# A fused gated-linear-attention and MoE kernel: the first six blocks taken as pairs with 384-byte loads, and a program order written out as a list

## The chip, the cores and the metric

The kernel runs on one core of one Trainium2 chip, in one launch. The metric is the device time of that core in microseconds (us); lower is better. A core has five engines that run side by side, each with its own queue of instructions that it executes in order: TensorE (PE in the profile; its weight loads are PEld), VectorE (DVE), ScalarE (ACT), GpSimd (POOL) and SyncE (SP). In this kernel SP issues all the DMAs. An instruction that must wait for another engine, or for a DMA, holds up everything behind it in its own queue.

## What is computed

There are 4 sequences of 768 tokens with 8 heads of 48 channels. For each head a 48x48 state is decayed per channel and updated at every token, and the output is read from it with the query:

```python
for t in range(S):
    state = alpha[:, :, t, :, None] * state + np.einsum('bhd,bhe->bhde', k[:, :, t], v[:, :, t])
    y[:, :, t] = np.einsum('bhd,bhde->bhe', q[:, :, t], state)
...
x = y.transpose(0, 2, 1, 3).reshape(B * S, H * D)    # 3072 x 384
h = x @ w_in                                         # w_in 384 x 2048
g = s * np.maximum(h, 0.0) ** 2 + b
out = g @ w_out                                      # w_out 2048 x 384
```

All inputs and the output are float32. The four attention inputs are 4.7 MB each and lie in memory as (batch, head, token, channel), so that the 48 channels of one head and token are 192 contiguous bytes. The two weights are 3.1 MB each.

## The kernel before

**Blocks.** The work is cut into 24 blocks of 128 tokens, 6 for each sequence, with one token per partition. Block n goes through a chain of steps. `load` brings a, q, k and v of the block, each as one DMA with 1,024 pieces of 192 bytes. `st_ln` takes the logarithm of alpha; `st_cum` sums it over the tokens by a product with a triangular matrix, and also gives the block's whole decay; `st_exp_b` and `st_exp_i` make the decay factors and their inverses; `st_qb` and `st_kb` multiply them into q and k; `st_vcast` rounds v to bfloat16. Blocks 0 to 7 are transposed by TensorE (`st_T`) and copied back by DVE (`st_Tcopy`); later ones are transposed by a DMA (`st_Tdma`). `st_KV`, `st_t1` and `st_snew` carry the state from block to block. `st_A` makes the 128x128 scores of each head, `st_mask` cuts them to the causal half, `st_y` multiplies them with v and adds what the state gives, and `st_yevac` copies the result to `xd_sb` as the input of the dense layers.

**Dense layers.** Blocks are put together in groups of one or two (`GROUPS`). `mm1` computes one unit of the first dense layer: 512 columns of PSUM, which for a group of two is two of the 16 slices of 128 hidden channels. `relu` (ACT) and `square` (DVE) take it to `gt_sb`. `mm2` computes a quarter of the second layer for one block: four products of 384 columns. After four quarters `oevac` (DVE) scales and adds the bias, and `ostore` writes the block out. The bias is `b` times the column sums of `w_out`, made from `colsum_part`, `colsum_add`, `bias_mm` and `bias_copy`. The weights come in as eight DMAs of 768 KB (`load_w_in`, `load_w_out`) through four staging buffers, and ACT rounds them to bfloat16 (`cast_w_in`, `cast_w_out`).

**Order.** `Schedule` takes each step as an operation with an engine, an expected duration, a priority and the buffers that it reads and writes; it plays them through and then emits the instructions in the order found. The list `LOADS` gives the order of the first loads and of the weights. `fill` puts products with zeros into the gaps on TensorE before the first `mm2`. There are five input buffers for each of a, q, k and v (`NIN`).

Of the kernel before, what the change touches and what calls it, by code (L numbers as in the profile page):

```python
# [14 lines left out]

VW = 144

GROUPS = [2, 1, 1, 2, 2, 2, 2, 2, 2, 2, 2, 2, 2]
UNIT = 0.756
LEAD = {1: 98.3, 2: 224.9, 4: 115.8}  # L20

NPE = 8

NAY = 9

RING = 12

NST = 4

TB = 1.02  # L30
TW = 2.15
FILL_GAP = 0.45

P_BM, P_CS, P_BMM = -5, -380.7, 485.1
P = dict(
    ln=-4.98, cum=7.29, eb=-25.15, ei=-13.19, vc=29.56, qb=-11.01, kb=-39.87, T=15.87,
    Tc=-9.38, KV=-36.89, t1=-9.91, sn=53.95, Ay=-1.22, A=-16.47, mk=-35.05, y=52.89,
    ye=4.82, m1=-13.73, re=-0.8, sq=-9.48, m2=-14.41, oe=20.18,
)

LOADS = ["k1", "q1", "a1", "i0", "k2", "v1", "i1", "a2", "i2", "q2", "i3", "v2", "a3", "q3", "k3", "o0", "v3", "a4", "o1", "o2", "k4", "o3", "q4", "z0", "v4"]

class Schedule:
    HOP = 0.05

    def __init__(self):
        self.ops = []
        self.writer = {}
        self.readers = {}

    def op(self, eng, dur, prio, fn, *args, r=(), w=(), lat=0.08, lock=False):
        me = len(self.ops)
        deps = set()
        for x in r:
            if x in self.writer:
                deps.add(self.writer[x])
        for x in w:
            if x in self.writer:
                deps.add(self.writer[x])
            deps.update(self.readers.get(x, ()))  # L60
        for x in r:
            self.readers.setdefault(x, []).append(me)
        for x in w:
            self.writer[x] = me
            self.readers[x] = []
        self.ops.append((eng, dur, prio, fn, args, deps, lat, lock))

    def run(self):
        n = len(self.ops)
        end = [None] * n  # L70
        begin = [None] * n
        left = [len(o[5]) for o in self.ops]
        users = [[] for _ in range(n)]
        for i, o in enumerate(self.ops):
            for d in o[5]:
                users[d].append(i)
        free = {}
        ready = {}
        port = 0.0
        for i, o in enumerate(self.ops):  # L80
            free.setdefault(o[0], 0.0)
            ready.setdefault(o[0], [])
            if not left[i]:
                ready[o[0]].append((0.0, i))
        todo = n
        while todo:
            best = None
            for e, items in ready.items():
                if not items:
                    continue  # L90
                f = free[e]
                at = [(max(a, f, port if self.ops[i][7] else 0.0), self.ops[i][2], i) for a, i in items]
                t = min(at)[0]
                _, i = min((p, i) for a, p, i in at if a <= t + 1e-9)
                if best is None or t < best[0]:
                    best = (t, e, i)
            t, e, i = best
            ready[e] = [x for x in ready[e] if x[1] != i]
            eng, dur, _, _, _, _, lat, lock = self.ops[i]
            begin[i] = t  # L100
            free[e] = t + dur
            end[i] = t + dur
            if lock:
                port = t + dur
            todo -= 1
            for u in users[i]:
                left[u] -= 1
                if not left[u]:
                    a = 0.0
                    for d in self.ops[u][5]:  # L110
                        same = self.ops[d][0] == self.ops[u][0]
                        x = end[d] + (0.0 if same and eng == "PE" else self.ops[d][6])
                        a = max(a, x + (0.0 if same else self.HOP))
                    ready[self.ops[u][0]].append((a, u))
        self.begin, self.end = begin, end
        return begin

    def emit(self, fill, until):
        begin = self.run()
        free = 0.0  # L120
        for i in sorted(range(len(self.ops)), key=lambda i: (begin[i], i)):
            eng, _, _, fn, args = self.ops[i][:5]
            if eng == "PE":
                if fn is until:
                    free = None
                if free is not None:
                    if free > 0.0:
                        fill(begin[i] - free, free)
                    free = self.end[i]
            fn(*args)  # L130
# [3 lines left out]
def kernel(  # L134
# [13 lines left out]
    ctx.enter_context(tc.manual_schedule())  # L148

    B, H, S, D = q.shape  # L150
    C = 128
    NCH = S // C
    NP = H // 2
    NBLK = B * NCH
    d_model = moe_w_in.shape[0]
    d_ff = moe_w_in.shape[1]
    NJ = d_ff // 128
    NIN = 5

    sb = ctx.enter_context(tc.tile_pool(name="sb", bufs=1))  # L160
# [235 lines left out]
    def st_snew(n):  # L396
        if n % NCH in (0, NCH - 1):
            return
# [321 lines left out]
```

## Time and profile before

| | before |
|---|---|
| time, median of 3 runs | 194.94 us (193.78 to 196.74) |
| time of the profiled execution | 193.93 us |
| its span, first to last instruction | 192.0 us |
| granted TensorE clock, mean | 0.991 |
| PE busy | 175.3 us |
| PEld busy | 126.7 us |
| DVE busy | 135.9 us |
| ACT busy | 109.5 us |
| POOL busy | 33.3 us |
| DMA, all queues | 34.44 MB |

The time of an execution is 1.9 us longer than the span that the profile shows. Busy time counts an instruction from its start to its end, and instructions of PE and PEld are pipelined: they overlap one another, so a PE that is busy all the time need not be at its peak. In the page, strips of 40 digits show the busy share of an engine in 40 equal slices of the span, in tenths. "SPq" is SP's queue of DMA issues: a long time there is an issue that was held up. A group of instructions is named by its line in the kernel, its engine, and "output<-input" in the names of the tiles.

### The profile page before, as it was taken

The numbers are of one execution on the slowest core, as the hardware profiler recorded it, in microseconds if no ns is written. First come the engines' busy times: TensorE is split into PE (matmuls) and PEld (weight loads), VectorE is DVE, ScalarE is ACT, GpSimd is POOL, SyncE is SP. The second block draws the span as 40 slices with busy tenths as digits, with TensorE's granted clock in tenths as the row PEclk, the third lists the DMA queues.
The fourth block names the chain that finished last, engine by engine and source line by source line (L and its number), as shares of the span: only waits on it lengthen the run. The fifth ranks groups of instructions, "written<-read, shape, count | busy, mean of one in ns | idle before, by whom it ended". The sixth has DMA issues, their size and how long they took to land.

```text
span 192.0 us, 5369 instructions
## 1 busy us (share of the span) xinstructions
PE 175.3 (91%) x2153; PEld 126.7 (66%) x2153; DVE 135.9 (71%) x256; ACT 109.5 (57%) x225; POOL 33.3 (17%) x60
## 2 busy tenths in 40 slices
PE   1877688879999999999999999999999999999992
PEld 0555467657677767777777766776766876777761
DVE  4643299989799898877689868587777786554421
ACT  3254789984357847767475754763663763654300
POOL 8402022103120431201122313011131131000000
PEclk9996999999999999999999999999999999999999
DMA  6989979999999999999999998897998895011112
GB/s 122 203 219 317 312 161 245 353 223 205 196 232 193 219 140 213 197 214 188 196 160 209 145 236 188 171 207 169 208 197 195 164 180 144 3 43 41 40 45 82
DMA packets 124218, 34.44 MB, mean 179 GB/s; under 512 B 117536, under 2 KB 122656, under 8 KB 124192
## 3 DMA queue, kind: packets, MB, share of 16 engines
q1 hardware_dynamic: 124192, 34.09, 82.6%
q8 instruction: 17, 0.28, 0.6%
q14 instruction: 9, 0.07, 0.1%
HBM read 25.17 MB, written 4.72 MB: 156 GB/s over the span
## 4 chain that ended last, share of the span: by engine, by line
PE 66%; DMA 14%; DVE 8%; SPq 7%; ACT 2%; issue 1%
PE o_ps L515 29%; PE h_ps L490 25%; PE py_ps L444 5%; DMA wst<-in_moe_w_in_dram 4%; DMA q_in<-in_q_dram 4%; SPq L194 4%; DMA wst<-in_moe_w_out_dram 3%; PE a_ps L406 3%; SPq L240 3%; DMA qkT<-qk 3%; DVE am L415 2%; PE py_ps L364 2%; PE ct_ps L306 1%; DVE gt L506 1%; ACT r L499 1%
## 5 line engine op out<-in xcount | busy, mean ns | idle before, releaser
L490 PE MATMUL h_ps<-xd,w_in_bf 128*128 128x256 bf16 (+1 forms) x624 | 74.8, 264 | 0.8 <-ACT r L499 0.5
L499 ACT ACTIVATE r<-h_ps 128x512 bf16<-128x512 f32 x96 | 56.5, 601 | 32.3 <-PE h_ps L490 22.8
L515 PE MATMUL o_ps<-w_out_bf,gt 128*128 128x384 bf16 x384 | 72.8, 326 | 2.0 <-ACT w_out_bf L261 2.0
L490 PEld LDWEIGHTS <-w_in_bf 128*128 128x128 bf16 x624 | 54.7, 98 | 10.8 <-issue 1.2
L506 DVE TENSOR_TENSOR gt<-r 128x512 bf16<-128x512 bf16 x96 | 43.5, 465 | 21.7 <-ACT r L499 21.1
L515 PEld LDWEIGHTS <-gt 128*128 128x128 bf16 x384 | 36.0, 98 | 21.2 <-issue 2.3
L415 DVE TENSOR_TENSOR am<-a_ps,mask 128x1024 bf16<-128x1024 f32 x24 | 29.3, 1220 | 1.6 <-PE a_ps L406 1.4
L327 POOL CAST vp<-v_in 128x384 bf16<-128x384 f32 x24 | 13.3, 553 | 95.0 <-DMA v_in<-in_v_dram 84.7
L526 DVE SCALAR_TENSOR_TENSOR o_sb<-o_ps,s_col,bias_w 128x384 f32<-128x384 f32 x24 | 14.8, 616 | 10.0 <-PE o_ps L515 9.6
L300 ACT ACTIVATE la<-a_in 128x384 bf16<-128x384 f32 x24 | 12.5, 521 | 14.1 <-DMA a_in<-in_alpha_dram 13.9
L400 POOL TENSOR_TENSOR s_st<-t,blast 128x384 bf16<-128x384 bf16 x16 | 14.5, 909 | 30.8 <-DVE t L389 23.0
L468 ACT ACTIVATE xd<-py_ps 128x384 bf16<-128x384 f32 x24 | 11.8, 491 | 13.0 <-PE py_ps L444 12.8
L338 DVE TENSOR_TENSOR qk<-k_in,binv 128x384 bf16<-128x384 f32 x24 | 13.4, 558 | 6.7 <-ACT binv L323 5.5
L333 DVE TENSOR_TENSOR qk<-q_in,b_s 128x384 bf16<-128x384 f32 x24 | 13.5, 564 | 5.2 <-ACT b_s L320 4.1
L320 ACT ACTIVATE b_s<-ct_ps 128x384 f32<-128x384 f32 x24 | 11.7, 488 | 6.8 <-PE ct_ps L311 6.7
L389 DVE TENSOR_TENSOR t<-py_ps,s_st 64x192 bf16<-64x192 f32 x32 | 11.3, 353 | 3.9 <-PE py_ps L364 3.2
L306 PE MATMUL ct_ps<-la,U_bf 128*128 128x384 bf16 x24 | 8.0, 334 | 6.3 <-ACT la L300 6.3
L323 ACT ACTIVATE binv<-ct_ps 128x384 f32<-128x384 f32 x24 | 11.8, 490 | 0.0
L311 PEld LDWEIGHTS <-la 128*128 128x128 bf16 x96 | 6.0, 97 | 7.7 <-issue 5.6
L406 PE MATMUL a_ps<-qkT 64*128 64x128 bf16 x192 | 9.8, 222 | 1.0 <-DVE qkT L373 0.7
L406 PEld LDWEIGHTS <-qkT 64*128 64x128 bf16 x192 | 5.5, 96 | 7.3 <-issue 4.3
L444 PE MATMUL py_ps<-am,vp 128*32 128x128 bf16 x384 | 9.8, 224 | 0.5 <-DVE am L415 0.5
(42 smaller groups left out, 108.1 us busy)
## 6 DMA issues: line engine op xcount, KB each, us to landing
a_in<-in_alpha_dram SPq DMA_DIRECT2D x24, 192.0 KB, 3.9
q_in<-in_q_dram SPq DMA_DIRECT2D x24, 192.0 KB, 3.9
k_in<-in_k_dram SPq DMA_DIRECT2D x24, 192.0 KB, 3.9
v_in<-in_v_dram SPq DMA_DIRECT2D x24, 192.0 KB, 3.7
out_dram<-o_sb SPq DMA_DIRECT2D x24, 192.0 KB, 2.6
wst<-in_moe_w_in_dram SPq DMA_DIRECT2D x4, 768.0 KB, 8.4
wst<-in_moe_w_out_dram SPq DMA_DIRECT2D x4, 768.0 KB, 7.0
qkT<-qk SPq DMA_TRANSPOSE x16, 3.7
```

The source lines that it names most:

```text
L327: nc.gpsimd.tensor_copy(out=vp_sb[n % 4].rearrange("a p (x d) -> a p x d", d=D)[:, :, 0:3:2, :], in_=v_in[n % NIN].rearrange("a (p e) d -> ...
L333: nc.vector.tensor_tensor(out=qk_sb[n % 3][:, 0, :, 0:D], in0=q_in[n % NIN], in1=b_sb[n % 2], op=ALU.mult)
L338: nc.vector.tensor_tensor(out=qk_sb[n % 3][:, 1, :, 0:D], in0=k_in[n % NIN], in1=binv_sb[n % 2], op=ALU.mult,)
L400: nc.gpsimd.tensor_tensor(out=s_sb[n % 3], in0=t1_sb[n % 2], in1=bl, op=ALU.mult)
L406: nc.tensor.matmul(out=a_ps[:, e, p, :], lhsT=qkT[64 * e : 64 * e + 64, 1, p, :], rhs=qkT[64 * e : 64 * e + 64, 0, p, :], start=True, stop ...
L415: nc.vector.tensor_tensor(out=am_sb[n % 2].rearrange("a e p t -> a (e p) t"), in0=a_ps.rearrange("a e p t -> a (e p) t"), in1=mask.unsquee ...
L444: nc.tensor.matmul(out=y_ps[32 * (x % 4) : 32 * (x % 4) + 32, x // 4, :], lhsT=(st[:, p, c0 : c0 + 32] if e is None else vp[:, p, c0 + 48 ...
L490: nc.tensor.matmul(out=hp[:, i * n : (i + 1) * n], lhsT=w_in_bf[:, kk, 128 * j : 128 * (j + 1)], rhs=xd_sb[g % 3][:, kk, 0:n], start=(kk = ...
L499: nc.scalar.activation(out=r_sb[w % 2], in_=h_ps[w % 2], func=AF.Relu)
L506: nc.vector.tensor_tensor(out=gt_sb[:, js[0] : js[0] + len(js), c0 : c0 + n], in0=r, in1=r, op=ALU.mult)
L515: nc.tensor.matmul(out=op[:, 0:d_model], lhsT=gt_sb[:, j, c0 : c0 + C], rhs=w_out_bf[:, j, :], start=(j == 0), stop=(j == NJ - 1),)
L526: nc.vector.scalar_tensor_tensor(out=ots, in0=o_ps[(x // 4) % 2][:, 0:d_model], scalar=s_col, in1=bias_w, op0=ALU.mult, op1=ALU.add,)
```

## The change

The scheduler is gone. The order of all instructions is given by `PROGRAM`, a string of 897 items such as `mm1.0.6.0` (unit 6 of group 0 into PSUM bank 0) or `re.0.6.0.0.ACT`, which also name the engine for many steps. The other parts of the change are these:

- Blocks 0 to 5 are taken as three pairs of 256 tokens. Partition p holds the tokens 2p and 2p+1, so that a load (`ld2`) has pieces of 384 bytes; it brings two blocks with 1,024 pieces. The first half of the partitions is then the first block of the pair, the second half the second block. The steps ending in 2 handle such a pair: sums, scores and outputs are split by token parity `s` and by block `c`, and products that belong to one block use 64 rows of TensorE's array.
- From block 6 on, all transposes are DMAs (`T1`); blocks 6 and 7 were transposed by TensorE before. The three pairs are transposed by TensorE.
- All groups have two blocks; before there were two groups of one.
- Input buffers hold six blocks for each of a, q, k, v (before five); `gt` holds eight blocks (before twelve). Two weight loads are staged in `gt` buffers (`STAGE_GT`).
- The weights are rounded by ACT, DVE and POOL, and the column sums made by POOL and DVE. Some of the relu steps run on DVE, some of the squares on ACT or POOL, four of the first multiplications on POOL.
- Zero products to fill gaps stand at four places, as `F.26`, `F.33`, `F.19` and `F.16`, with 120 columns (before 45 products with 256 columns).
- A block of a pair is stored with two DMAs (`st`).

```diff
-GROUPS = [2, 1, 1, 2, 2, 2, 2, 2, 2, 2, 2, 2, 2]
-NPE = 8
-RING = 12
-LOADS = ["k1", "q1", "a1", "i0", "k2", "v1", "i1", "a2", "i2", "q2", "i3", "v2", "a3", "q3", "k3", "o0", "v3", "a4", "o1", "o2", "k4", "o3", "q4", "z0", "v4"]
-class Schedule:
...
+NPAIR = 3
+GROUPS = [2, 2, 2, 2, 2, 2, 2, 2, 2, 2, 2, 2]
+NIN = 6
+RING = 8
+STAGE = {0: 0, 1: 1, 2: 2, 3: 3, 6: 0, 7: 1}
+STAGE_GT = {4: 2, 5: 3}
+CUM_IN_H = [1]
+PROGRAM = """
+ld2.a.0 c_act c_U2 c_la.1 c_la.0 ld2.a.1 c_zeros ld2.v.0 c_half c_qk.0 ld2.q.0 c_t1.0 c_qk.1 c_mask2
+ld2.k.1 ld2.k.0 c_s.0 ld2.q.1 ln2.0 c_s.1 ld2.q.2 c_t1.1 ld_i.3 F.26 cum2.0.0 c_ident ld2.v.1 ln2.1
+cum2.0.1 c_U c_ones blk2.0 c_vp.1 eb2.0.1 cum2.1.0 c_s.2 ei2.0.0 cum2.1.1 c_vp.0 blk2.1 ei2.0.1
+vc2.0.1.POOL el2.0 vc2.0.0.DVE eb2.1.0 mul2.q.0.1.DVE ei2.1.0 eb2.1.1 el2.1 mul2.k.1.0.DVE ei2.1.1
+eb2.0.0 mul2.k.1.1.DVE mul2.q.0.0.DVE mul2.k.0.0.DVE F.33 T2.0.0 mul2.k.0.1.DVE mul2.q.1.1.POOL KV2.0
+ld1.k.7 Tc2.0.0.ACT ld_i.1 T2.0.1 t1.0 mul2.q.1.0.POOL ld_i.2 ld2.a.2 t1.1 ld1.k.6 Tc2.0.1.DVE ld_i.0
+ld2.k.2 sn.1.DVE F.19 A2.0.0 ld_o.0 A2.0.1 ci.3.POOL mk2.0.0 ld1.a.6 ld2.v.2 mk2.0.1 F.16 T2.1.0
+vc2.1.1.ACT vc2.1.0.POOL T2.1.1 Tc2.1.0.ACT Tc2.1.1.DVE y2.0 A2.1.0 ye.0.DVE ye.1.ACT A2.1.1 mk2.1.0
+KV2.1 ci.1.ACT mm1.0.6.0 t1.2 mm1.0.7.1 re.0.6.0.0.ACT ld_o.3 mk2.1.1 sn.2.POOL ld1.a.7 re.0.7.1.1.ACT
...
+sn.4.POOL ld1.q.6 sq.1.7.1.ACT mm1.1.6.1 mk2.2.1 ld1.q.8 cp.3.POOL re.0.1.0.1.ACT ld_bs co.1.DVE y2.2
+cp.1.POOL sq.0.1.1.DVE ye.5.ACT ye.4.DVE mm2.0.0 co.2.ACT ld1.v.8 re.1.6.1.1.DVE cum1.6 ld1.a.10
+mm1.2.5.0 sq.1.3.0.POOL cp.2.DVE ld1.q.7 mm1.2.0.1 ld1.a.8 ei1.6 ca.2.3.DVE ld1.v.6 ca.0.1.POOL mm2.0.1
...
+cum1.8 bc re.2.1.0.0.ACT mm1.2.7.1 vc1.6.POOL mul1.q.6.DVE eb1.8 mm1.2.4.0 oe.0 T1.6 sq.2.1.0.ACT KV1.6
...
+sn.7.POOL ld1.v.13 mk1.6 mm2.2.3 st.1 ei1.9 mm2.3.0 ld1.k.9 oe.2 ld1.q.9 cum1.10 Ay.7 ld1.k.11 eb1.10
...
+mm2.22.2 mm2.22.3 oe.22 st.22
+"""
...
+    def ld2(x, m):
+        b, c = 2 * m // NCH, 2 * m % NCH
+        nc.sync.dma_start(
+            out=whole(ins[x], m).rearrange("a s e -> a (s e)").rearrange("a (h f) -> a h f", h=H),
+            in_=src[x][b, :, c * C : (c + 2) * C, :].rearrange("h (p s) d -> p h (s d)", s=2),
+        )
...
+    def cum2(m, s):
+        l = whole(la, m)
+        for i in range(2):
+            nc.tensor.matmul(
+                out=b_ps(m, s)[:, 0 : H * D],
+                lhsT=U2x if i > s else U2,
+                rhs=l[:, i, :, 0:D],
+                start=(i == 0),
+                stop=(i == 1),
+            )
...
+        for p in range(NP):                                  # KV2
+            for s in range(2):
+                for c in cs:
+                    r = slice(64 * c, 64 * c + 64)
+                    nc.tensor.matmul(
+                        out=(py_ps, ct_ps)[c][:, 96 * p : 96 * p + 96],
+                        lhsT=kb[r, s, 128 * p : 128 * p + 128],
+                        rhs=v4[r, s, p, 0:3:2, :],
+                        start=(s == 0),
+                        stop=(s == 1),
+                    )
...
+        for p in range(NP):                                  # A2
+            for e in range(2):
+                r = slice(64 * e, 64 * e + 64)
+                for c in range(2):
+                    t = slice(64 * c, 64 * c + 64)
+                    nc.tensor.matmul(
+                        out=dst[t, e, 128 * p : 128 * p + 128],
+                        lhsT=T[r, s, 1, p, t],
+                        rhs=T[r, :, 0, p, t],
+                        start=True,
+                        stop=True,
+                    )
...
+        for i, (p, e, x) in enumerate(OWN):                  # y2
+            c0 = 32 * x - 96 * p + 48 * e
+            for s in range(2):
+                for c in range(2):
+                    r = slice(64 * c, 64 * c + 64)
+                    nc.tensor.matmul(
+                        out=y_out((py_ps, ct_ps)[c], x),
+                        lhsT=v2[r, s, p, c0 : c0 + 32],
+                        rhs=a2[r, s, e, p, :],
+                        start=(i < 4 and s == 0),
+                        stop=(i >= 12 and s == 1 and c not in states),
+                    )
...
+    def re(g, u, w, i, eng="ACT"):
+        if eng == "ACT":
+            nc.scalar.activation(out=r_sb[i], in_=h_ps[w], func=AF.Relu)
+        else:
+            nc.vector.tensor_scalar(
+                out=r_sb[i], in0=h_ps[w], scalar1=0.0, scalar2=None, op0=ALU.max
+            )
...
+    def sq(g, u, i, eng="DVE"):
+        r = r_sb[i].rearrange("a (j t) -> a j t", j=4 // GROUPS[g])
+        if eng == "ACT":
+            nc.scalar.activation(out=unit_out(g, u), in_=r, func=AF.Square)
+        else:
+            on(eng).tensor_tensor(out=unit_out(g, u), in0=r, in1=r, op=ALU.mult)
...
+    def F(n):
+        for _ in range(n):
+            nc.tensor.matmul(
+                out=h_ps[1][:, 392:512], lhsT=zeros[:, 0:128], rhs=zeros[:, 0:120], start=True, stop=True
+            )
+
+    ops = dict(locals())
+    for item in PROGRAM.split():
+        name, *args = item.split(".")
+        ops[name](*(int(x) if x.lstrip("-").isdigit() else x for x in args))
```

In the items of `PROGRAM`, `ld1`, `ld2`, `ld_i`, `ld_o` and `st` are loads and stores; `ci` and `co` round a quarter of `w_in` or `w_out`; `cp` and `ca` make the column sums; `bm`, `bmm` and `bc` the bias; `ln`, `cum`, `blk`, `eb`, `ei`, `el`, `vc`, `mul`, `KV`, `t1`, `sn`, `A`, `mk`, `y`, `ye` are the attention steps in the order told above, with 2 for a pair and 1 for a single block; `T2` and `Tc2` transpose a pair; `Ay.n` is the scores of block n followed by the output of block n-1; `re`, `sq`, `oe` are `relu`, `square` and `oevac`.

## The prediction

> **What bounds the kernel now.** I read the page first, for the busy shares over the span.
>
> ```profile
> span 192.0 us, 5369 instructions
> PE 175.3 (91%) x2153; PEld 126.7 (66%) x2153; DVE 135.9 (71%) x256; ACT 109.5 (57%) x225; POOL 33.3 (17%) x60
> ...
> PE   1877688879999999999999999999999999999992
> ...
> DMA  6989979999999999999999998897998895011112
> ...
> q1 hardware_dynamic: 124192, 34.09, 82.6%
> ```
>
> PE never pauses after the tenth slice (48 us); before, it is short of work while the DMA engines are already full. So the middle is bound by PE, the first quarter by loads. The chain of waits says which loads:
>
> ```profile
> 8.80 4.49 SPq L240
> 13.87 8.26 DMA wst<-in_moe_w_in_dram
> 22.15 1.49 ACT w_in_bf L248
> ...
> 25.47 6.15 DMA wst<-in_moe_w_out_dram
> ...
> 34.60 8.07 DMA q_in<-in_q_dram
> ...
> 47.73 2.11 PE o_ps L515 x12
> ...
> 55.64 1.31 PE h_ps L490 x12
> ...
> 180.67 7.81 PE o_ps L515 x48
> ```
>
> Until 47.7 us the path hangs on weights and inputs in turn; then products follow one another to the end. The last rows are prices: a unit of `mm1` is 0.655 us (1.31 for two), a quarter of `mm2` 0.65 (7.81 for twelve). The windows say how much PE lacks:
>
> ```profile
> 20.00:25.00 5.00, 3.85 (x38) 3.08 (x38) 1.94 (x4) 4.30 (x8) 0.00 (x0) 1.00 0.97 264
> 40.00:45.00 5.00, 4.17 (x63) 3.37 (x61) 4.56 (x9) 3.03 (x5) 0.95 (x1) 1.00 0.95 180
> 60.00:80.00 20.00, 20.00 (x275) 14.64 (x273) 18.32 (x36) 13.41 (x31) 6.00 (x8) 1.00 1.02 191
> ```
>
> The columns are length, busy time (count) of PE, PEld, DVE, ACT and POOL, clock, DMA share, GB/s. Around 20 us DVE is idle; by 40 us DVE and DMA are full and PE is not.
>
> **PE's sum before.** From the timeline, a block costs 0.35 us (`st_cum`), 0.17 (`st_KV`), 0.33 (`st_A`), 0.51 (`st_y`; 0.34 without a state), 0.45 more if PE transposes it. The first `mm1` starts at 21.0, after two blocks. From there: `mm1` 88 x 0.655 + 8 x 0.75 (groups of one) = 63.6; `mm2` 96 x 0.65 = 62.4; 22 blocks 29.1; six transposes 2.7; bias 1.4; together 159.2. PE ends at 188.5, so 8.3 us are waits and filling, nearly all before 50 us; 3.5 us of evacuation and store end the span.
>
> **DMA prices.** The packet records give means of 15.6 ns for 192 bytes, 27.4 for the 256 of a transpose, 73.5 for 1,536 and 97.5 for 2,048. Over 16 engines that is 1.00 us for a load of 1,024 packets, 1.75 for a transpose, 0.59 for a store, 2.35 for a weight. Packets overlap a little:
>
> ```profile
> 3.71 0.52 ACT L300 ACTIVATE la<-a_in 128x384 bf16<-128x384 f32 x1 [1.70 <-DMA a_in<-in_alpha_dram]
> 9.34 0.52 ACT L300 ACTIVATE la<-a_in 128x384 bf16<-128x384 f32 x1 [3.52 <-DMA a_in<-in_alpha_dram]
> ```
>
> Six loads land between these two logarithms, 0.94 us each, so I scale all by 0.95: load 0.95, transpose 1.67, store 0.56, weight 2.23. Data starts at 1.8 us, and a landing is seen 1.0 after its last byte.
>
> **Pair loads.** No packet of 384 bytes is in the trace. Below: the count of packets sets the price, 0.95 us a pair. Above: the bytes, two loads, 1.9. The straight line from 192 to 1,536 gives 23.9 ns, x 64 packets an engine x 0.95 = 1.45; I take this, being between two measured sizes. Twelve pair loads then save 12 x (1.90 - 1.45) = 5.4 us, in the stretch where the queue is the bound.
>
> The Trainium skill (DMA: Bandwidth & Descriptors, Specifications) asks for 512 bytes for line rate and has smaller transfers read, modified and written; 384 would stay on the bad side with 192. If that means the same price per byte, the pairs gain nothing, and the sum below is 5.4 us longer. The trace has no size between 256 and 1,536 that could show such a step.
>
> **When the dense layers start.** The sixth pair load (k of pair 0) lands at 1.8 + 6 x 1.45 + 1.0 = 11.5. The exponentials (eight of 0.39) are done by 10. Then one after another: two multiplications 1.0, `KV2` 0.5, `t1` twice 1.45, `Tc2` 0.6, `A2` 0.5, two masks 2.4, `y2` 1.6, `ye` 0.5, `KV2` 0.5 with handovers: 20.8. `ci.3` is on POOL from 16 to 18, covered by the masks. So the start is where it was, but four blocks are nearly through instead of two. At 0.95 a pair it would be 19.4 (the exponentials limit), at 1.9, 23.6.
>
> **What else moves.** Eighteen relus go to DVE: at least 0.42 us each (its square of the same tile), at most 0.83 (0.62 for 384 columns from PSUM, by size); I take 0.65, nearest the second: 12 us. Squares leave DVE: 15 to ACT (a relu's 0.60 at most), 8 to POOL (0.83 by size, 1.1): 23 x 0.46 = 11 off DVE. That is even, and hidden in the middle by what PE has queued, since DVE there keeps 8% free in the fullest window; in the ramp DVE's work is part of the walk below. Groups of one go: 8 x (0.75 - 0.655) = 0.8 off PE, in its sum. New waits stand on SP: `ld1.k.7` waits for the last multiplication of pair 0 (12.5 us), with all weights but one behind it, but at that time the queue still has three transfers (to 16 us); `ld_o.2` waits for `ci.0` on POOL (29), and SP comes to it at about 33; `ld_o.0` and `ld_o.1`, staged in `gt`, only hold up the squares of group 2, which come after 41. At nothing, all of them; without that cover, each us on SP is one of the queue. The sixth input buffer lets loads run further ahead, which only helps.
>
> **64-row products.** `y2` has 64 products of 64x32 and 24 for the states. Now 16 of 128x32 take 0.33 us, by overlapping. Below: the same 21 ns and less for the states, 1.5; above: nothing overlaps, 53 ns (128 columns at the rate of 0.65 us for 1,536), 88 x 53 = 4.7. I take 1.6, since the products stay in four column groups; a pair is then 0.64 (`cum2`) + 0.2 + 0.9 (`T2`) + 0.5 + 1.0 (`A2`) + 1.6 = 4.8 (upper end 8.7).
>
> **PE's sum after.** From the first `mm1`: 96 x 0.655 = 62.9; 62.4; 18 single blocks 23.5; bias 1.4; `y2` of pair 1, 1.6; pair 2, 4.6: 156.4. Walking the list to `y2.2` by hand, I find 3 us of waits: `re.0.3` on DVE behind `mk2.1.1`, `co.0` waiting for a weight, `cum2.2` behind `ye.3`. 20.8 + 156.4 + 3 + 3.5 = 183.7.
>
> **The queue's sum after.** `A1.6` needs `T1.6`, queued behind 12 pair loads (17.4), eight weights (17.8) and 17 loads (16.2), itself 1.67: 53.1 + 1.8 + 1.0 = 55.9. What PE has from there (72 `mm1`, 86 `mm2`, 18 blocks less their first sums) is 125.3: end 55.9 + 125.3 + 3.5 = 184.7. The same for `Ay.19`: 17.4 + 17.8 + 72 x 0.95 + 14 x 1.67 + 14 x 0.56 = 134.8, at 137.6; left are 24 `mm1`, 33 `mm2` and five blocks, 43.1: 184.2. So queue and PE bind together. The two added transposes (3.3 us of queue, 0.9 off PE) are in it. A transpose holds SP until its multiplications are done, and the loads behind it wait; the queue's own backlog hides that, and where it is short each us counts. I add 1.0. Double stores add six issues of about 0.4 us to SP, under cover of the same backlog. Longer filling on PE has no price: it stands where PE waits.
>
> Span 184.7 + 1.0 = 185.7. The execution before is 1.9 above its span: 187.6. Its median (194.94) stands 1.0 above the profiled 193.93: **188.6**.
>
> **Rivals.** *Pairs are priced by bytes.* For it: the rule above; against: the straight line. Every bound on the queue moves by 12 x 0.45 = 5.4: 194.0, no change that shows.
>
> *GpSimd comes too late.* It gets two weight casts, one more of `w_out`, three column sums and one addition, four multiplications and eight squares. After `ld_o.3` lands (about 35): `co.3`, `sn.4`, `cp.3`, `cp.1`, `sq`, `ca.0.1`, 9.1 us by its rows (cast 0.50 per 384 elements, product of two inputs 0.83), to 44; then 0.9 on DVE, and `bmm` stands at 46 in PE's queue with all products behind it. The reserve is 1 us. Against: the median cast is undisturbed. For it:
>
> ```profile
> L327 POOL CAST vp<-v_in x24: 502/507/952, 6.3 to 159.3; 128x384 bf16<-128x384 f32 x24
> ```
>
> The 952 ns came beside DVE's two-input additions. At 1.9 times, `bmm` is 7 us late: 195.6, slower than before; it decides from about 1.7 times on. The Trainium skill (GPSIMD Engine Reference, Key points) says that the two share their interfaces to SBUF, and that VectorE is about twice as fast.
>
> *The 64-row products don't overlap.* For it: each is half the array; against: the overlap now. Three pairs x 3.9 = 12 us of PE, of which filling hides some 3: 197.
>
> **Chances.** Forecast 0.64, bytes 0.14, GpSimd 0.13, products 0.09. Two per cent is about what a measurement of this kernel tells from no change: 191.0 and 198.8. Faster: 0.58 from the forecast and 0.02 from the bytes. Same: 0.06, 0.11, 0.05 and 0.03. Slower: the rest, 0.15. The low end takes pair loads at 0.95, where PE's chain holds it (19.4 instead of 20.8, no idle queue): 183.5. The high end takes in the first two rivals: 196.5. The forecast's own range is 184 to 192.
>
> **What would show it.** Right: packets of 384 bytes near 24 ns; the first `mm1` at 20 to 22; PE with waits of 3 to 6 us between 20 and 60, then almost none; last transpose near 145; PE's end about 6 us earlier. Wrong: PE waiting for `qkT` or `ct_ps` all along the middle (the queue is slower), or `bmm` waiting for `colsum` near 46 (GpSimd), or `y2` over 2.5 us.

## The result, and the profile after

The changed kernel takes 205.46 us (median of four runs, 203.74 to 206.63) where the kernel before takes 194.36 (193.54 to 196.74): 1.058 times as long, with a 95% interval of 1.046 to 1.070. The forecast was 188.6, with a range of 183.5 to 196.5. It was wrong in sign and by 17 us.

The page of the changed kernel, in the parts shown of before:

```profile
span 203.0 us, 5563 instructions
PE 179.6 (88%) x2292; PEld 129.8 (64%) x2292; DVE 141.3 (70%) x247; ACT 105.4 (52%) x211; POOL 58.0 (29%) x84
...
PE   5689898496899999699999999999998999998872
...
DMA  6999999647967999979999999999973722010211
```

TensorE now has holes up to the seventeenth slice (86 us), a smaller one in the thirty-first, and a thinner end. The strip of the DMA engines, which was nearly full up to 48 us, has a hole too, in the slices from 36 to 46 us. The windows, with the columns as before (length, PE, PEld, DVE, ACT, POOL, clock, DMA share, GB/s); the last row runs from the first `mm1` to TensorE's end:

```profile
40.00:45.00 5.00, 4.22 (x51) 3.00 (x50) 4.00 (x6) 3.06 (x6) 2.84 (x3) 0.56 0.30 60
60.00:80.00 20.00, 19.11 (x209) 13.08 (x208) 16.35 (x26) 8.19 (x20) 6.38 (x7) 1.00 0.94 191
22.73:199.00 176.27, 162.79 (x1974) 115.71 (x1970) 128.66 (x220) 94.80 (x194) 47.09 (x49) 0.98 0.75 159
```

The same last row of the kernel before:

```profile
21.04:188.47 167.43, 162.94 (x2016) 118.22 (x2014) 125.76 (x236) 101.06 (x211) 25.87 (x37) 1.00 0.84 177
```

Length less PE's busy time is its idle time: 4.5 us before, 13.5 after. So the change of 10.5 us in TensorE's end splits into a start that is 1.7 later and 9.0 of added waits; its busy time stayed where it was. The chain of waits of the changed kernel, through the ramp:

```profile
32.06 1.71 DVE w_out_bf L306
...
35.05 1.96 DVE gt L697
...
37.88 1.44 PE h_ps L668 x6
...
40.84 1.44 PE h_ps L668 x6
...
45.26 2.08 DVE w_out_bf L306
...
49.58 1.43 DVE colsum L322
...
52.83 0.82 PE h_ps L668 x6
...
54.95 1.29 PE o_ps L336 x4
```

Before, this stretch of the chain hung on DMAs. Now it hangs mainly on VectorE, until the bias products (`bmm`, L336) at 54.8, which stood at 45 before and were forecast at 46. The three pieces of about 2 us (both casts of `w_out`, and `gt<-r`, a square) are operations that take 0.95 and 0.42 us in e2 below. And TensorE's own timeline at the end:

```profile
184.31 2.76 PE L702 MATMUL o_ps<-w_out_bf,gt 128*128 128x384 bf16 x16
187.78 2.76 PE L702 MATMUL o_ps<-w_out_bf,gt 128*128 128x384 bf16 x16 [0.71 <-DVE o_sb L711]
...
196.89 2.11 PE L702 MATMUL o_ps<-w_out_bf,gt 128*128 128x384 bf16 x12 [0.71 <-DVE o_sb L711]
```

Four times (at 187.1, 190.5, 192.7 and 196.2) the last products wait 0.71 us for an evacuation (`oe`, L711). Before, 48 products followed one another there without a gap.

### The profile page after: what moved, and what is told of

Same layout as the page of the kernel before. It is cut to its first block, busy times and chain, and to the rows that moved or that the text cites. A ratio compares the mean times of both kernels' runs of the same rounds, so it can differ in the third digit from the quotient of the medians.

```text
span 203.0 us, 5563 instructions
## 1 busy us (share of the span) xinstructions
PE 179.6 (88%) x2292; PEld 129.8 (64%) x2292; DVE 141.3 (70%) x247; ACT 105.4 (52%) x211; POOL 58.0 (29%) x84
## 4 chain that ended last, share of the span: by engine, by line
PE 62%; DVE 16%; DMA 9%; SPq 4%; issue 4%; ACT 3%; DVEq 0%
PE o_ps L702 26%; PE h_ps L668 20%; DMA qkT<-qk 4%; DMA a_in<-in_alpha_dram 4%; PE py_ps L600 4%; SPq L262 4%; PE a_ps L578 3%; DVE o_sb L711 2%; DVE am L462 2%; DVE gt L697 2%; DVE w_out_bf L306 2%; DVE r L680 2%; PE h_ps L733 2%; DVE qk L548 2%; PE py_ps L565 1%
## 5 line engine op out<-in xcount | busy, mean ns | idle before, releaser
L668 PE MATMUL h_ps<-xd,w_in_bf 128*128 128x256 bf16 x576 | 74.5, 277 | 5.0 <-DVE r L680 3.9
L668 PEld LDWEIGHTS <-w_in_bf 128*128 128x128 bf16 x576 | 55.9, 99 | 18.4 <-issue 6.7
L678 ACT ACTIVATE r<-h_ps 128x512 bf16<-128x512 f32 x78 | 46.3, 597 | 26.4 <-PE h_ps L668 20.5
L697 DVE TENSOR_TENSOR gt<-r 128x512 bf16<-128x512 bf16 x73 | 35.9, 499 | 18.6 <-ACT r L678 18.0
L646 POOL TENSOR_TENSOR s_st<-t,blast 128x384 bf16<-128x384 bf16 x15 | 13.5, 900 | 46.5 <-DVE t L636 39.5
L711 DVE SCALAR_TENSOR_TENSOR o_sb<-o_ps,s_col,bias_w 128x384 f32<-128x384 f32 x24 | 14.8, 616 | 15.3 <-PE o_ps L702 15.0
L587 DVE TENSOR_TENSOR am<-a_ps,U 128x1024 bf16<-128x1024 f32 x18 | 22.0, 1220 | 0.8 <-PE a_ps L578 0.6
L695 ACT ACTIVATE gt<-r 128x512 bf16<-128x512 bf16 x15 | 9.5, 633 | 9.0 <-DVE r L680 8.9
L680 DVE TENSOR_SCALAR r<-h_ps 128x512 bf16<-128x512 f32 x18 | 12.2, 685 | 1.8 <-ACT gt L695 0.6
L697 POOL TENSOR_TENSOR gt<-r 128x512 bf16<-128x512 bf16 x8 | 10.0, 1250 | 9.5 <-DVE r L680 9.5
L733 PE MATMUL h_ps<-zeros 128*128 128x120 bf16 x94 | 8.4, 273 | 3.3 <-ACT binv L386 1.8
L733 PEld LDWEIGHTS <-zeros 128*128 128x128 bf16 x94 | 7.7, 130 | 3.4 <-issue 1.9
L536 ACT ACTIVATE binv<-ct_ps 128x384 f32<-128x384 f32 x18 | 8.7, 485 | 1.7 <-PE ct_ps L524 1.7
```

The costliest lines, as they stand in the source:

```text
L587: nc.vector.tensor_tensor(out=half_of(am, n).rearrange("a e p t -> a (e p) t"), in0=a_ps.rearrange("a e (p t) -> a (e p) t", t=128), in1=U ...
L646: on(eng).tensor_tensor(out=s_sb[n % 3], in0=t1_sb[n % 2], in1=bl.unsqueeze(2).to_broadcast([128, NP, 96]), op=ALU.mult,)
L668: nc.tensor.matmul(out=h_ps[w][:, i * n : (i + 1) * n], lhsT=w_in_bf[:, kk, 128 * j : 128 * (j + 1)], rhs=xd_sb[g % 3][:, kk, 0:n], start= ...
L678: nc.scalar.activation(out=r_sb[i], in_=h_ps[w], func=AF.Relu)
L680: nc.vector.tensor_scalar(out=r_sb[i], in0=h_ps[w], scalar1=0.0, scalar2=None, op0=ALU.max)
L697: on(eng).tensor_tensor(out=unit_out(g, u), in0=r, in1=r, op=ALU.mult)
```

## The experiments

Four suspicions came out of these views. **A**: `o_ps`, the output sums of `mm2`, was two tiles of one PSUM bank and is one tile of two banks now (the list of the change ahead of the prediction leaves this out), and products into one bank wait for the evacuation of the other. **B**: VectorE is held by GpSimd, whose busy time rose from 33.3 to 58.0 us. **C**: SP stood from 32.9 to 42.4 us at one load. **D**: 33 zero products ahead of the first transposes cost time. The low clock (0.56 from 40 to 45 us, 0.76 in the five before) I took for a consequence of TensorE's holes; in e2, e12 and e5 below it reads 1.00 throughout the ramp. It has a price of its own: in the chain above, six products of `mm1` take 1.44 us at 37.9 and at 40.8, and 0.82 at 52.8. What lowers the clock was not tested, and no run separates its price from B. All ratios are to runs of the kernel before on the same chip, with 95% intervals; gains are in per cent of the kernel before. The profiled lines are of one execution each.

**One tile or two (e1).**

```diff
-    o_ps = ps.tile([128, 2, 512], FP32, name="o_ps")
+    o_ps = [ps.tile([128, 512], FP32, name=f"o_ps{i}") for i in range(2)]
```

The mask of a pair that reads both tiles becomes two operations, one for each tile.

> The changed kernel with o_ps as two tiles of one bank each (mask of the second half as two VectorE operations of 512 columns). Theory A (one tile for both banks makes every mm2 wait for the evacuation of the other bank): the four TensorE stalls of 0.71 us behind oe at the end go, TensorE ends 2.8 us sooner there, and one to three us more come from the ties along the middle: 201 us (199.5 to 203). Rival (the evacuation is late for another reason, and the stalls stay or move): 205 within 1. The start up to 60 us is as it was.

Measured: 200.9 us, ratio 1.034 (1.026 to 1.041), a gain of 2.4%. TensorE's waits for evacuations (total, times, longest) in the changed kernel,

```profile
PE o_ps L702 <- DVE o_sb L711: 5.8, 7, 1.7
```

and with two tiles:

```profile
PE o_ps L711 <- DVE o_sb L720: 0.4, 2, 0.2
```

The four stalls at the end are gone: TensorE ends 3.5 us sooner (195.5), while `bmm` still starts at 54.3. A holds.

**GpSimd relieved (e2).** Eleven items change their engine. Gathered from their places in the program, they are:

```diff
-cp.0.POOL cp.1.POOL cp.3.POOL ca.0.1.POOL co.3.POOL ci.0.POOL mul2.k.2.0.POOL
+cp.0.DVE  cp.1.DVE  cp.3.DVE  ca.0.1.DVE  co.3.ACT  ci.0.ACT  mul2.k.2.0.DVE
-sq.1.4.1.POOL sq.0.0.0.POOL sq.1.3.0.POOL mul2.k.2.1.POOL
+sq.1.4.1.ACT  sq.0.0.0.ACT  sq.1.3.0.ACT  mul2.k.2.1.DVE
```

> The changed kernel with GpSimd's eleven large operations after the first mm1 (casts, column sums, squares, two multiplications of the third pair) on VectorE and ScalarE instead. Theory B (a VectorE operation with two SBUF inputs is held until GpSimd's operation ends): VectorE's squares of 35 to 48 us go from 1.3-2.0 to about 0.42 us, colsum adds take 0.95 on VectorE, bmm starts at 46 to 49 instead of 54.8, TensorE's gaps between 35 and 50 shrink from 4.5 to under 2 us, the time is 199 us (196 to 202.5). Rival (VectorE and ScalarE are full there in any case, the work only moves): bmm at 53 or later, 205 or more.

Measured: 202.5 us, ratio 1.041 (1.031 to 1.050); `bmm` at 49.4. VectorE in the changed kernel, and the GpSimd operation that its square meets:

```profile
34.98 2.02 DVE L697 TENSOR_TENSOR gt<-r 128x512 bf16<-128x512 bf16 x1
37.13 0.69 DVE L680 TENSOR_SCALAR r<-h_ps 128x512 bf16<-128x512 f32 x1
...
34.59 2.12 POOL L322 TENSOR_TENSOR colsum<-gt 128x768 f32<-128x768 f32 x1
```

and VectorE with GpSimd relieved:

```profile
34.45 0.69 DVE L680 TENSOR_SCALAR r<-h_ps 128x512 bf16<-128x512 f32 x1
35.17 0.43 DVE L697 TENSOR_TENSOR gt<-r 128x512 bf16<-128x512 bf16 x1
```

The square ends just after GpSimd's sum ends (34.98 + 2.02 = 37.00, after 34.59 + 2.12 = 36.71). The relu, which reads PSUM, has its 0.69 us either way. VectorE has more operations now, and `bmm` comes 5.4 us sooner all the same. B fits. The total gained less, 1.7%: TensorE's idle time between 60 and 160 us rose from 4.8 to 7.0.

**The held load (e3).** `ld1.a.13` goes from behind `ld_o.2` to just ahead of `ld1.v.13`. In this run, and in e5 to e10 below, `ln1.13` stands ahead of the moved load, so block 13 takes the alpha of block 7 and waits for no load.

> The changed kernel with the one load ld1.a.13 moved in SP's queue from behind ld_o.2 to just ahead of ld1.v.13. Theory C (this load's wait for ln1.7 holds SP for 9 us and every load behind it): SP issues on after 32.9 us, the 40 to 45 stretch has a DMA share near 0.9 instead of 0.30, A1.6 starts near 57 instead of 63.6, the time is 202 us (200 to 204). Rival (the bias chain through GpSimd ends last there, the loads wait for nothing that counts): loads earlier, bmm still at 54 to 55, 205 within 1.

Measured: 206.3 us, ratio 1.061 (1.052 to 1.070), and `bmm` at 54.6. The queue went on:

```profile
33.95 4.92 SPq L262 DMA_DIRECT2D q_in<-in_q_dram  x2
38.91 3.34 SPq L297 DMA_DIRECT2D b_col<-in_moe_b_dram  x1
```

The loads were out earlier and nothing came of it: the chain through VectorE ended last. The queue was not free, though: the next three loads held SP until 42.3, and the DMA share from 40 to 45 us was 0.53 (0.30 in the changed kernel), where near 0.9 was expected. So moving this load gains nothing, and C falls in that form; what an unhindered queue would give, this run doesn't show.

**The zero products (e4).** `F.33` is deleted.

> The changed kernel without the group of 33 zero products ahead of the first transposes (F.33); the other three groups stay. Theory D (they run from 10.1 to 13.5 us while the operand of T2.0.0 is ready at 11.1): T2.0.0 about 2.3 us sooner, first mm1 at 20.4 instead of 22.7, the time 203.3 us (202 to 204.5) if that carries to the end. Rival (TensorE's clock is lower without them, or another wait takes their place): first mm1 at 22 or later, 205 within 1; or the first mm1 is 2 us sooner and the ramp's later waits (GpSimd, SP) give it all back: 205.

Measured: 205.1 us, ratio 1.056 (1.048 to 1.064). In the changed kernel the group looked expensive, with the first transposes behind it at 13.36, although their operand was ready at 11.1:

```profile
10.11 3.46 PE L733 MATMUL h_ps<-zeros 128*128 128x120 bf16 x33 [1.80 <-ACT binv L386]
...
15.23 0.61 PE L418 MATMUL a_ps<-ident,qk 128*128 128x128 bf16 x8 [0.66 <-ACT qkT L304]
15.68 1.16 PE L733 MATMUL h_ps<-zeros 128*128 128x120 bf16 x19
```

Without it:

```profile
13.16 1.01 PE L418 MATMUL a_ps<-ident,qk 128*128 128x128 bf16 x8 [0.36 <-ACT qkT L304]
13.96 2.10 PE L733 MATMUL h_ps<-zeros 128*128 128x120 bf16 x19
```

The first transposes start 2.35 us sooner, at 11.01, but the next take 1.01 us where they took 0.61, and the 19 zero products 2.10 where they took 1.16. The first `mm1` is only 0.85 sooner (21.88), and by `bmm` (54.6) even that is gone. So the rival of D holds: the products had to run for a while before they ran fast. The other profiled executions agree: the second group of transposes takes 1.01 us in e5, e9, e10 and e13, which lack `F.33`, and 0.61 in e1, e2, e3 and e12, which have it.

**A and B together (e12), and all four (e5).**

> Two changes at once: o_ps as two tiles, and GpSimd's eleven large operations on VectorE and ScalarE. If A and B are independent, their gains (4.5 us and 2.9 us of medians) add: 198 us (196.5 to 199.5). If the ties of o_ps only used slack that the late ramp gives (or the other way round), less: 200 or more. SP is still held by ld1.a.13 until about 39.

> All four at once: o_ps as two tiles, GpSimd relieved, ld1.a.13 later, no F.33. Theory C in its second form (the held queue costs nothing while the bias chain on VectorE ends last, but does once that chain is 5 us shorter): 1 to 3 us less than with the first two alone, 196 us (194 to 198), TensorE's idle time between 60 and 100 under 2 us. Rival (the loads are late for another reason, the order of SP's queue along the middle): as with the first two alone, 198 within 1.

Measured: 1.022 (1.017 to 1.027) with A and B, 1.020 (1.015 to 1.025) with all four. A alone took 2.4% off, B 1.7%, both 3.6%: within their intervals, they add. C and D add nothing that can be told, so C's second form falls too.

**The 384-byte pieces (e6).** From the version with all four:

```diff
+        for s in range(2):
             nc.sync.dma_start(
-                out=whole(ins[x], m).rearrange("a s e -> a (s e)").rearrange("a (h f) -> a h f", h=H),
-                in_=src[x][b, :, c * C : (c + 2) * C, :].rearrange("h (p s) d -> p h (s d)", s=2),
+                out=in2(x, m)[:, :, s, :],
+                in_=src[x][b, :, c * C : (c + 2) * C, :].rearrange("h (p s) d -> s p h d", s=2)[s],
             )
```

> The version with all four, and each pair load as two transfers of 192-byte pieces (same bytes, same places, twice the packets). If the 384-byte pieces are worth what the profile of before suggests (0.95 us for one block's load of 1024 packets, so 1.9 us for a pair against about 1.2 us): the six loads of the first two pairs land 3 to 5 us later, first mm1 at 24 to 26, the time 3 to 5 us longer. Rival (the bytes set the pace): first mm1 within 1 us of the version with all four, same time within 1.

Measured: ratio 1.055 (1.046 to 1.065), 3.5% more than with 384 bytes, the first `mm1` at 26.9 instead of 22.1. (The clock reads 0.88 from 15 to 27 us in this execution, so part of both may come by way of it.) The windows with pieces of 384 bytes:

```profile
5.00:10.00 5.00, 3.12 (x24) 1.67 (x23) 2.24 (x3) 3.96 (x12) 2.95 (x10) 1.00 1.17 325
```

and of 192:

```profile
5.00:10.00 5.00, 3.26 (x24) 1.73 (x23) 0.44 (x1) 3.10 (x9) 2.89 (x10) 1.00 1.08 211
```

The DMA engines are full in both (a share above 1: packets overlap), and move 325 GB/s or 211 (354 or 205 in the five us after). Forecast were 5.4 us for this part of the change; undone, it costs 0.035 x 192.4 = 6.8.

**GpSimd beside VectorE, by itself (e7).** Sixteen items `pl`, each `colsum[3] = colsum[2] + colsum[1]` on GpSimd, between 66 and 131 us, into the version with all four.

> The version with all four, and sixteen additional GpSimd additions of two 768-column SBUF operands, ahead of every second mm1 of the groups 3 to 7 (their result is read by nothing). Theory B (VectorE's SBUF-to-SBUF operations wait for the end of GpSimd's): VectorE's squares and multiplications that meet one take 1 to 2 us instead of 0.42 and 0.55, operations that read PSUM (relu, mask, evacuation) stay at their length; VectorE's busy time rises by 10 us or more; the time rises by 1 to 5 us as VectorE has some 20 us to spare along the middle. Rival (GpSimd and VectorE only share bandwidth, each is slowed a little): squares stay under 0.8 us, time within 1 us.

Measured: 209.9 us, ratio 1.090 (1.084 to 1.096), 14 us more for work that nobody reads. VectorE's groups without them (mean ns after the busy time):

```profile
L706 DVE TENSOR_TENSOR gt<-r 128x512 bf16<-128x512 bf16 x73 | 33.0, 459 | 21.5 <-ACT r L687 20.9
L596 DVE TENSOR_TENSOR am<-a_ps,U 128x1024 bf16<-128x1024 f32 x18 | 21.9, 1219 | 1.9 <-PE a_ps L587 1.7
```

and with them:

```profile
L709 DVE TENSOR_TENSOR gt<-r 128x512 bf16<-128x512 bf16 x73 | 41.7, 582 | 18.5 <-ACT r L690 18.1
L599 DVE TENSOR_TENSOR am<-a_ps,U 128x1024 bf16<-128x1024 f32 x18 | 21.9, 1219 | 1.2 <-PE a_ps L590 1.1
```

Squares, with both inputs in SBUF, grew by 8.7 us in all, the multiplications of k and q, likewise, by 6.5 (11.3 to 17.8) and 5.2 (11.3 to 16.5); the masks, with one input in PSUM, by nothing. The damage in time was three times the most that I expected, since I had counted on VectorE's slack. Part of it may come by way of the clock, which reads 0.97 between 60 and 160 us and 1.00 without the additions; the squares' length does not, since the masks keep theirs under the same clock. B holds. The Trainium skill (SBUF — State Buffer, Who interferes with whom) says that VectorE and GpSimd share one pair of ports under an exclusive lock: a VectorE instruction with two SBUF inputs contends with a GpSimd one that reads SBUF, and so can a cast in a fast mode, where the one that issues first has the pair for its whole instruction and the other is blocked. The lines agree, the casts of `w_out` included (0.95 us alone, 1.71 and 2.08 in the chain above).

**The rest: stores, order of loads, zeros (e8, e9, e10).** From the version with all four. In e8 most stores go four SP items later; e9 also moves nine loads of alpha five items ahead; e10 instead deletes `F.26`, `F.19` and `F.16`.

> The version with all four, and most stores of the blocks 0 to 15 four SP instructions later, behind the loads and transposes that followed them. Theory G (TensorE's remaining 5.3 us of waits after 55 us come from SP's queue, where a store waiting for its evacuation, 27.7 us in nine waits, holds loads and transposes): those waits of TensorE fall to 3 us or less, the time by 1.5 to 2.5 us, to 193.5-194.5 where the version with all four takes 195.8. Rival (the transposes are late because VectorE multiplies late): waits on qkT stay, 195.8 within 0.7.

> As the last, and the nine loads of alpha for the blocks 14 to 22 five SP instructions earlier. Theory G: the wait of TensorE's cum1 for la (1.24 us near 143) goes too, another 0.5 to 1.2 us less, 193 (192 to 194). Rival: another load of the same block, pushed back by these, ends last instead; no change within 0.5 against the last.

> The version with all four, and no zero products at all (F.26, F.19 and F.16 gone too). Theory H (they buy speed: in the profiles the same transposes take 1.03 us for a group of eight early on and 0.61 later, the same A2 products 0.64 and 0.42): the first pairs run at the long durations up to the first mm1, which starts 0.5 to 2 us later than 22.1, and the time is 0.5 to 2 us longer. Rival (they only fill waits): first mm1 and time within 0.4 us.

Measured: 1.016 (1.006 to 1.025), 1.011 (1.003 to 1.019) and 1.023 (1.017 to 1.030), beside 1.020. The intervals overlap: e8 is inconclusive, and the small gain that e9 points to is not shown. In e10 the first `mm1` came at 23.36, 1.2 us later, and sixteen transposes ahead of it took 1.87 us instead of 1.06, as theory H has it; the total is not told apart.

**With the order of block 13 kept (e5b), and loads in the order of use (e13).** e5b puts `ld1.a.13` behind `ld1.v.7`; e13 adds the later stores and sorts the loads after `bmm` by their first reader.

> The version with all four, with ld1.a.13 behind ld1.v.7 and so still ahead of ln1.13 (in the runs where it stood just ahead of ld1.v.13, ln1.13 came before it and took block 7's alpha for block 13, without waiting for a load). If that displacement counted for nothing in the time: 1.018 to 1.022 of before, as with it. Rival (the load of a.13 and the wait of ln1.13 cost something in their place): 1.025 or more.

> As the last, stores four SP instructions later, and the loads after bmm put into the order in which their blocks' first reader uses them (the places in the queue stay). If TensorE's waits at 60 to 120 us (4 us) come from loads issued in the wrong order (k of block 10 lands behind k of 11 and 12, and VectorE waits 1.65 us for it): under 2 us of waits after 55, 1.000 to 1.012 of before. Rival (what is late is the transpose behind VectorE's multiplications, whatever the order of loads): 1.012 to 1.02.

Measured: 1.024 (1.016 to 1.033) and 1.014 (1.005 to 1.023). The misplaced `ln1.13` of the earlier runs made no difference that can be told. In e13 TensorE's waits for `la` and for evacuations are gone from the list of waits; what is left after 60 us is, but for 0.4 us, transposes, more than the 2 us that I expected:

```profile
PE a_ps L587 <- DMA qkT<-qk: 3.9, 5, 0.9
```

**Column sums on TensorE (e14, e15).** From e13 and from e5b: `cp`, `ca` and `bm` go, and `bmm` becomes sixteen products of ones with the cast `w_out`, scaled by `b_col` in `bc`.

> As the last, and the column sums of w_out (four cp and three ca of 0.95 us and bm on VectorE, four bmm products of 0.49 us) made by sixteen products of ones with the cast w_out on TensorE, scaled by b_col on the way out. Theory I (after GpSimd is relieved VectorE is what the ramp waits for: 4.8 to 5.0 us busy in every 5 from 30 to 50): 6.7 us less on VectorE, 16 x 0.16 - 4 x 0.49 = 0.6 us more on TensorE, and the ramp is 2 to 5 us shorter: 0.975 to 0.995 of before. Rival (ScalarE's casts and relus, 4.0 to 4.6 in every 5, bound it next to VectorE): 1 us or less against the last.

> The column sums on TensorE with SP's order as it was (the first of these four, with that one edit). Theory I: 2 to 5 us less than the first of these four; if the middle's late loads take the gain back (an earlier ramp only waits longer for them), less than 1.5 us less, and TensorE's waits between 60 and 120 grow by what the ramp gained.

Measured: 1.017 (1.010 to 1.023) and 1.025 (1.015 to 1.035), no gain over e13 and e5b. The windows of e13:

```profile
25.00:50.00 25.00, 19.90 (x360) 14.95 (x360) 22.92 (x38) 21.75 (x42) 2.82 (x3) 1.00 0.93 246
59.40:146.00 86.60, 82.58 (x1017) 59.56 (x1016) 66.30 (x119) 46.90 (x101) 20.03 (x25) 1.00 1.00 193
60.00:160.00 100.00, 95.59 (x1204) 68.99 (x1204) 78.18 (x140) 55.02 (x118) 23.70 (x30) 1.00 0.94 179
```

and of e14:

```profile
25.00:50.00 25.00, 21.42 (x374) 16.25 (x373) 18.63 (x34) 22.99 (x44) 2.83 (x4) 1.00 0.92 243
60.00:160.00 100.00, 93.53 (x1186) 67.38 (x1184) 75.72 (x135) 54.12 (x117) 22.38 (x29) 1.00 0.92 177
```

VectorE was relieved in the ramp (18.6 us busy instead of 22.9) and TensorE gained 1.5 us there. It lost 2.1 in the middle. So relieving VectorE in the ramp does not move the end, and theory I falls.

**Later products (e16, e17).** From e14: each `Ay.n` from 9 on behind the next `mm1` or `mm2`; in e17 five of them behind one more.

> The version with the column sums on TensorE and the loads by use, and each Ay.n from 9 on (products of block n with its transpose, then y of the block before) behind the mm1 or mm2 that followed it, still ahead of mk1.n. Theory J (after the ramp is mended, TensorE's waits are for transposes that land 0.3 to 1.5 us behind the place of A1 in its order, 5.5 us in six; there is work in the queue to put ahead): those waits fall to 2.5 us or less and the time by 2 to 3 us, to 1.000 to 1.007 of before. Rival (the blocks' own chain, load to transpose to mask to y, has the length of the wait, so later products make the next block later): no gain, 1.012 to 1.02.

> As the last, and five of them (blocks 9, 14, 15, 18, 22) behind one more mm2, which passes mk1.n and ye too. Theory J: another 0.5 to 1 us less, 0.997 to 1.005 of before. Rival: as the last or longer.

Measured: 1.018 (1.013 to 1.023) and 1.028 (1.021 to 1.034). In e16 the waits for transposes fell from 5.5 to 2.5 us, as expected, and the time did not fall; in e17 it rose. The rival fits: a block that is multiplied later makes the next thing later. In e17 the waits for transposes after 60 us are gone, and TensorE waits 3.4 us for `xd`, the copied outputs, instead (0.4 in e16).

**One tile in the kernel before (e18).** The last run puts theory A alone into the kernel before:

```diff
-    o_ps = [ps.tile([128, 512], FP32, name=f"o_ps{i}") for i in range(2)]
+    o_both = ps.tile([128, 2, 512], FP32, name="o_ps")
+    o_ps = [o_both[:, i, :] for i in range(2)]
```

> The kernel before, with the two banks of o_ps taken as halves of one tile, as the changed kernel has them; nothing else. Theory A alone: each mm2 that starts or stops in one bank while the evacuation of the other stands ahead in the order waits for it (0.7 us each time); the stalls appear at the end (two to four, 1.4 to 2.8 us) and where VectorE is behind along the middle: 1.010 to 1.025 of before. Rival (the stalls only cost in the changed kernel's order, with its two blocks of a pair finishing together): within 0.7% of before.

Measured: 199.2 us, ratio 1.033 (1.026 to 1.039): 6.4 us for two lines that change nothing but the waits, more than I expected. Its list of waits (total, times, longest) has a row that the kernel before lacks:

```profile
PE o_ps L516 <- DVE o_sb L527: 4.1, 8, 0.7
```

From the first `mm1` on TensorE is idle for 10.6 us, 6.1 more than before, and 4.1 of that are these waits. Two more rows are each 1.0 us longer than before, those for the cast of `w_out` (3.0) and for a multiplication (1.4), both in the first 43 us; whether the tie brings them is not shown. No version of the changed kernel beat the kernel before; the best were e9 and e13, 1.1 and 1.4% behind it.

## Why the prediction was wrong, point by point

**The sum, term by term.** Forecast: first `mm1` at 20.8, 156.4 of products, 3 of waits, 3.5 behind TensorE's end, by PE's own sum. Measured: 22.7, 162.8 (busy), 13.5 and 4.0. The waits are the failure: the forecast had 3 us of them, all in the ramp, and two causes that it had priced at nothing, or within a reserve, brought most of the rest.

- *A step that is missing: the output tile.* The declaration of `o_ps` was in the diff, and I gave it no price, not even nothing. e1 puts it at 2.4% of the kernel before, 4.7 us; e18 at 6.4 us by itself. By the medians it is the largest single cause that the runs show; the intervals of e1 and e2 overlap.
- *"GpSimd comes too late", the rival with 0.13.* Its place was right: `bmm` was late, at 54.8 instead of 46, and 5.4 us of that go in e2 (it said 7). Its mechanism was not: I asked how much slower GpSimd gets beside VectorE, but the six GpSimd operations that I had summed at 9.1 us took 9.6. The harm goes mainly the other way, to VectorE's squares, casts and multiplications, the engine of the ramp, which I priced at their undisturbed durations. The sign that I named didn't come either: TensorE does not wait for `colsum`, it waits before that for VectorE's relus (3.5 us in three waits). e2 puts the whole at 1.7%, 3.4 us, with the clock in it. The 952 ns outlier that I showed fits this meeting of the two engines; I gave the median more weight than it bore, since GpSimd had little to do before.
- *"Longer filling on PE has no price."* Wrong in the view (the group held the transposes for 2.3 us), right in the sum (e4). I took all zero products as filler; the transposes behind them in e4 and e10 show that they also bring the products that follow up to speed.
- *Waits on SP "at nothing, all of them".* No run shows a price for them. I missed `ld1.a.13`, the longest of the ramp; moving it (e3) gained nothing either.
- *Pair loads at 1.45 us.* Mis-sized on the safe side: in the changed kernel the first two loads are seen 1.21 us apart (`ln2` at 4.30 and 5.51), which is 1.21 x 16 / 1,024 = 19 ns a packet. The packets themselves were near the straight line, 22.4 ns in the mean of their 12,288 records where it gave 23.9, but they overlap more than my factor of 0.95 allows: the DMA share is 1.16 between 5 and 10 us. The bytes rival falls by e6. The 512 bytes that the Trainium skill asks for at line rate (DMA: Bandwidth & Descriptors, Specifications) don't put 384 and 192 on one level: in e6's windows and those beside them the rate is 325 and 354 GB/s with 384 bytes, 211 and 205 with 192.
- *The first `mm1` at 20.8.* It was 22.7. In executions whose early products ran fast (e2, e9) it was at 20.6, in those of e1, e5, e5b, e12 and e13 at 21.7 to 22.5: the walk was right for fast products, and the timeline of before had shown both speeds (the sum over tokens 0.48 us at 4.3 and 0.32 at 20.7).
- *64-row products at 1.6 us for `y2`.* They overlapped: in the changed kernel's timeline the 64 of `y2.0` run from 19.80 to 20.74, and the twelve with the state take 0.31 more. The third rival falls.
- *Relu 0.65, squares 0.60 and 1.1, casts 2.0 (four times 0.50).* Measured 0.69, 0.63 and 1.25, 1.46 on GpSimd: near enough. Undisturbed unit prices were not the trouble.
- *Products, 156.4.* In e13, at full clock, TensorE is busy for 158.5 us from the first `mm1` on, against 162.9 in the kernel before. Without the 1.0 us of zero products in the latter the saving of work is 3.4 us, and 2.8 was forecast: it was real. What takes it back is idle time: 9.7 us in e13, 4.5 before.
- *The queue's sum.* It had `A1.6` at 55.9 and `Ay.19` at 137.6, 81.7 us apart. In e13 they are at 59.4 and 146.0, 86.6 apart. The window of e13 shown above has a DMA share of 1.00 over that stretch, so the queue was full there on the average. Without the factor of 0.95, which I took from six loads near the start, my sum gives 81.7 / 0.95 = 86.0. So the factor is the term that was mis-sized: early on packets overlap by more than it says, in the middle they don't. The sign that I had named for a slower queue came: TensorE waits for `qkT` along the middle. It fits that neither a faster ramp (e14, e15) nor another place for the products (e16, e17) helped. That the queue sets the end of e13 is argued from these rows and stays open: the kernel before has the same share between 60 and 146 us, at 191 GB/s, with 0.7 us of idle time on TensorE, and no run took bytes off the queue in the middle.

By ratios, A and B account for 3.6 of the 5.8%, and the order of loads and stores (e5b to e13) perhaps for another 1, though their intervals overlap; the rest, 1.4 in e13, is not settled. It is also open why no version shows the gain of some 3% that was forecast; the queue's rows above are the best lead. One rival stands untested: the changed kernel also puts two blocks into one tile in many of its SBUF buffers, and no run takes these apart.

## What to carry to other kernels

When a diff merges two buffers into one tile, price every wait that the tile's readers and writers may now share, before any instruction is counted: two banks in one tile cost 3% here, with no operation changed. Moving arithmetic to an idle GpSimd isn't free when VectorE is working from SBUF to SBUF at that time: ask what each VectorE operation reads, and add GpSimd's durations to VectorE's. And a long wait in a queue (SP's 9 us) can go without a gain that shows, while four of 0.7 us at the end of the kernel cost all that they show.

## What the runs showed of the hardware that I had not expected

- A VectorE operation with both inputs in SBUF that starts during a GpSimd operation ends just after it (2.02 us instead of 0.42 for a square), and one that reads PSUM isn't touched (a relu of 0.69 either way). GpSimd's sixteen additions of 1.9 us cost 14 us of time (e7).
- The same zero products took 105 ns each in one execution (33 in 3.46 us) and 57 in another (1.89 us, in e2), with the granted clock shown as 1.00 in both, and the first sum over tokens 0.48 or 0.32. The Trainium skill knows the two speeds (TensorE: Matmul & The Clock Gate, What's actually happening: half rate until TensorE has been busy for a while, and the count of slow products varies from run to run). The column of the profile does not show them here.
- With a DMA share above 1 in both, pieces of 384 bytes moved 325 and 354 GB/s in two windows and pieces of 192 bytes 211 and 205 (e6). The overlap of packets isn't one number: the share is 1.16 where pair loads run, and 1.00 in the full middle of e13.
